# Windowed attention and SwiGLU on one core: blocks of tokens cut as 4 x 256 and 4 x 512 in place of 3 x 256, 4 x 512 and 256

## The chip, the cores and the metric

The kernel runs on one core of a Trainium2 chip. The metric is the device time of one execution in microseconds (us), lower is better. Before the change it is 239.15 us, the median of 5 runs (238.95 to 239.62). The engines are named as the profile names them: PE (TensorE matmul, with its weight loads PEld), DVE (VectorE), ACT (ScalarE), POOL (GpSimd) and SP (SyncE). POOL and SP issue the DMAs here.

## What is computed

Sliding-window attention with four sink tokens, and then a SwiGLU block over all tokens. Batch 4, 8 heads, 768 tokens, head size 64; model width 512, inner width 1536.

```python
scores = scale * np.matmul(q, k.transpose(0, 1, 3, 2))
is_sink = pos[None, :] < int(n_sink)                 # n_sink = 4
in_window = (rel >= 0) & (rel < int(window))         # window = 128
scores = np.where(is_sink | in_window, scores, -1e9)
a = softmax(scores)                                  # over the keys
x = (a @ v).transpose(0, 2, 1, 3).reshape(B * S, H * D)   # 3072 x 512
g = x @ w_gate
out = (g * sigmoid(g) * (x @ w_val)) @ w_out         # 3072 x 512, float32
```

## The kernel before

**Groups and blocks.** The attention works on groups of 256 tokens, three to a batch, so g = 0 to 11; `c = g % 3` is the place in the batch, and a group with c = 0 has no earlier window and no sink part. The SwiGLU block works on blocks of tokens, `SIZES`, with `OFF` their first tokens. Before, block 0 is group 0, block 1 group 1, block 2 group 2, blocks 3 to 6 are pairs of groups from (3, 4) to (9, 10), and block 7 is group 11.

**Units.** The program is a list of units that `weave` runs in order. A `gate` unit makes a `pg` (gate) and a `pv` (value) projection of 512 columns into PSUM, `project` at L417. ACT takes the tanh (`th`, L432), DVE makes `u` (L438) and `ht` (L440, L444). For a block of 512 tokens a unit is one of 12 chunks of the inner width, and `pg` is 4 matmuls of 512 columns. For a block of 256 tokens it is two chunks side by side, and `pg` is 8 matmuls of 256 columns. Blocks 0 and 1 share one `xT` and one `ht` tile, so that from chunk 6 on they run as one block "01" of 512 tokens. The weights arrive chunk by chunk, which is why the first block begins narrow. A `down` unit makes 128 output tokens in 12 matmuls (`pd`, L475); ACT copies them out of PSUM (`ot`, L480), and SP issues the store (L483).

**Attention steps** are hung into units by `slots`: a pair ((units), [steps]) says in which unit a step stands. In a gate unit the steps stand between `pg` and `pv`, in a down unit they are spread between its matmuls. What they leave for DVE or SP to do (`later`) is issued after the step or at the unit's end.

- `load_nat(g)`, `load_v(g)`: POOL loads q, k and v of a group with four and two DMAs of 128 KB. `NV` is both. From group 4 on `nat` has a single buffer, so the next group's loads wait until the crossbar has read the last.
- `xbar(g)`: four transposes of q and k by DMA, issued on SP (L259), for groups 4 to 11. `step_TN(g, i, j)` does the same on PE for groups 2 and 3 (`pn`, L245), and ACT or DVE copies the result out of PSUM.
- `step_S(g, p2)`: half of a group's scores, 12 matmuls (8 where c = 0) into four PSUM banks; four exponentials on ACT (L299), two masks on DVE. `step_K(g)`: scores of the sink tokens (`pk`), with one exponential `es`.
- `step_PV(g, j, hh)`: a quarter of a group's attention output (`o`, L355); the first quarter carries the sinks' four matmuls (L335) where c > 0. DVE normalizes to `xn` (L363, L369).
- `step_X(g, j)`: the transpose of 128 tokens of `xn` into the block's `xT`. Groups in `PEX` do it on PE (`px`, L396) with a copy by ACT or DVE (L399, L403). The others do it by DMA on SP (L391), "the crossbar".
- `step_ks(b)`, `step_vsb(b)`: the sink tokens' keys and values of a batch.

**Order.** Each engine runs its instructions in the order in which the program lists them, and SP's queue too: crossbar transposes of q and k, of `xn`, and the stores of the outputs stand in one line there. PSUM has eight banks for everything, `xT` three buffers, `ht` two.

**The first weave** has 24 units: group 0's and 1's narrow gates (units 0 to 5), six wide gates "01" (6 to 11), six narrow gates of block 2 (12 to 17), two down units each of blocks 0, 1 and 2 (18 to 23). Within it stand the attention of groups 2, 3 and 4, the transposes `xbar` 4 to 6 and the loads up to group 7. Then each of blocks 3, 4 and 5 is a weave of 12 gate and 4 down units in which `pair` hangs two groups of attention: (5, 6), (7, 8), (9, 10). The last weave holds blocks 6 and 7, with group 11's attention in block 6.

Of the kernel before, what the change touches and what calls it, by code (L numbers as in the profile page):

```python
# [8 lines left out]
BF16 = mybir.dt.bfloat16  # L9
# [5 lines left out]
def kernel(  # L15
# [12 lines left out]
    nc = tc.nc  # L28
    P = 128
# [7 lines left out]
    DMC = DM // P  # L37
    DFC = DF // P
    NP2 = H // 2
    GC = S // 256  # L40
    NG = B * GC
    SIZES = [256, 256, 256, 512, 512, 512, 512, 256]
    assert sum(SIZES) == NTOK and NG == 12
    OFF = [sum(SIZES[:i]) for i in range(len(SIZES))]
    PEX = (0, 1, 2, 4)

    VS = 72
    FCH = [2] * 6
# [4 lines left out]
    def pool(name, bufs, psum=False):  # L53
        if psum:
            return ctx.enter_context(
                tc.tile_pool(name=name, bufs=bufs, space=bass.MemoryType.PSUM))
        return ctx.enter_context(tc.tile_pool(name=name, bufs=bufs))
# [11 lines left out]
    xtp = pool("xtp", 3)  # L69
# [8 lines left out]
    def bank(shape, dtype, name):  # L78
        return psum.tile(shape, dtype, tag="b", name=name)
# [24 lines left out]
    def load_nat(g):  # L104
        b, c = divmod(g, GC)
        x = (natp if g > 3 else rowp).tile(
            [P, 2, 2, DM], BF16, tag="nat" if g > 3 else "rows", name="nat")
        for i, src in ((0, k), (1, q)):
            for j in range(2):
                t0 = c * 256 + j * P  # L110
                nc.gpsimd.dma_start(  # L111
                    x[:, i, j].rearrange("p (h d) -> p h d", d=D),
                    src[b, :, t0:t0 + P].rearrange("h p d -> p h d"))
        nats[g] = x
# [22 lines left out]
    def load_out(i):  # L137
        n = DFC // 4
        t = wpool.tile([P, n, DM], BF16, tag=f"wo{i}", name="wo")
        nc.gpsimd.dma_start(  # L140
            t, moe_w_out[i * n * P:(i + 1) * n * P].rearrange("(c p) f -> p c f", p=P))
        wos.append(t)
# [6 lines left out]
    vcl = const.tile([P, B - 1, D + 1], FP32)  # L149
# [57 lines left out]
    kTs, qTs, es_t, e_t, xns, xTs = {}, {}, {}, {}, {}, {}  # L207
    later = []

    def flush():  # L210
        for f in later:
            f()
        later.clear()
# [159 lines left out]
        else:  # L373
            later.append(dve)

    def dense(t, c, n):
        return t[:, 0:c * n].rearrange("p (c n) -> p c n", c=c)

    def step_X(g, j, evict="v"):
        t0 = g * 256 + j * P  # L380
        tb = max(i for i in range(len(SIZES)) if OFF[i] <= t0)
        off = t0 - OFF[tb]
        if tb == 0 and off == 0:
            xTs["01"] = xtp.tile([P, DMC, 512], BF16, tag="xT", name="xT")
            xTs[0], xTs[1] = (xTs["01"][:, :, 256 * i:256 * (i + 1)] for i in range(2))
        elif tb > 1 and off == 0:
            xTs[tb] = dense(xtp.tile([P, DMC * 512], BF16, tag="xT", name="xT"),
                            DMC, SIZES[tb])
        if g not in PEX:
            def sp():  # L390
                nc.sync.dma_start_transpose(xTs[tb][:, :, off:off + P], xns[g, j])  # L391
            later.append(sp)
            return
        pt = bank([P, DMC, P], BF16, "px")
        for i in range(DMC):
            nc.tensor.transpose(pt[:, i], xns[g, j][:, i * P:(i + 1) * P], ident)  # L396

        if evict == "a":
            nc.scalar.copy(out=xTs[tb][:, :, off:off + P], in_=pt)  # L399
            return  # L400

        def dve():
            nc.vector.tensor_copy(out=xTs[tb][:, :, off:off + P], in_=pt)  # L403
        if evict == "now":
            dve()
        else:
            later.append(dve)

    hts = {}
# [11 lines left out]

    def gate_a(tb, f):
        if tb not in hts:
            n = SIZES[tb]
            t = hpool.tile([P, DFC * 512], BF16, tag="ht", name="ht")
            hts[tb] = dense(t, DFC, n)
            if tb == 0:
                hts["01"] = t.rearrange("p (b c n) -> p b c n", b=2, c=DFC)
                hts[1] = t[:, DFC * n:2 * DFC * n].rearrange("p (c n) -> p c n", c=DFC)
        pg = project(wgs, tb, f, "pg")  # L430
        th = tpool.tile([P, 512], FP32, tag="th", name="th")
        nc.scalar.activation(th, pg, AF.Tanh, scale=0.5)  # L432
        return pg, th

    def gate_b(tb, f, pg, th):
        pv = project(wvs, tb, f, "pv")
        u = upool.tile([P, 512], BF16, tag="u", name="u")
        nc.vector.scalar_tensor_tensor(u, th, 1.0, pg, op0=ALU.add, op1=ALU.mult)  # L438
        if tb == "01":
            nc.vector.tensor_tensor(  # L440
                hts[tb][:, :, f], *(x.rearrange("p (b n) -> p b n", b=2) for x in (u, pv)),
                op=ALU.mult)
            return
        nc.vector.tensor_tensor(  # L444
            hts[tb][:, f:f + 512 // SIZES[tb]].rearrange("p a n -> p (a n)"), u, pv,
            op=ALU.mult)
# [42 lines left out]
    def gates(tb):  # L489
        return [(gate, tb, f) for f in range(0, DFC, 512 // SIZES[tb])]  # L490

    def downs(tb):
        return [(down, tb, t) for t in range(SIZES[tb] // P)]

    def A(fn, *a):
        return lambda: fn(*a)

    def TN(g, evict="av"):
        return [A(step_TN, g, i, j, evict) for j in range(2) for i in range(2)]

    def Ss(g):
        return [A(step_S, g, p2) for p2 in range(2)]

    def PVs(g):
        return [A(step_PV, g, j, hh) for hh in range(2) for j in range(2)]

    def Xs(g):
        return [A(step_X, g, j) for j in range(2)]

    def K(g):  # L510
        return A(step_K, g)

    def weave(us, slots):
        assert all(i < len(us) for i in slots)
        for i, (fn, tb, x) in enumerate(us):
            fn(tb, x, slots.get(i, []))
# [7 lines left out]
    def slots(*pairs):  # L524
        sl = {}
        for at, steps in pairs:
            for i, step in zip(at if isinstance(at, tuple) else (at,) * len(steps),
                               steps):
                sl.setdefault(i, []).append(step)
        return sl  # L530
# [79 lines left out]
    load_gate(4)  # L610
    load_gate(5)
    for i in range(4):
        load_out(i)
    step_T(1, 0, 0, "a")
    step_T(1, 0, 1, "a")
# [15 lines left out]
    step_S(1, 1)  # L631
    later[:0] = masks1
    flush()
    load_nat(3)
    load_v(3)
    nc.gpsimd.memset(vcl, 0.0)
    nc.gpsimd.memset(vcl[:, :, D:D + 1], 1.0)
    load_sinks(vcl, 1, B)

    g0, g1, g2 = gates(0), gates(1), gates(2)  # L640
    us = [g0[0], g0[1], (alone, 0, 0), (both, g0[2][1:], g1[0][1:]), g1[1],
          g1[2], *((gate, "01", f) for f in range(6, DFC)),
          *g2, *downs(0), *downs(1), *downs(2)]

    def L(*fs):
        def f():
            for x in fs:
                x()
        return f

    def NV(g):
        return L(A(load_nat, g), A(load_v, g))
# [5 lines left out]
        ((4, 4, 5, 5), TN(2)), ((6, 7), Ss(2)), (6, [K(2)]),  # L658
        ((8, 8), PVs(2)[:2]), (9, [A(step_PV, 2, 0, 1, "a"), A(step_PV, 2, 1, 1, "a")]),
        ((10, 11), [A(step_X, 2, 0, "a"), A(step_X, 2, 1, "a")]),  # L660
        (11, [NV(4), lambda: nc.gpsimd.tensor_copy(out=vcl[64:128], in_=vcl[0:64])]), ((14, 14, 15, 15), TN(3, "aa")),
        (15, [A(xbar, 4)]), (15, [NV(5)]), (19, [A(xbar, 5)]), (19, [NV(6)]),
        (23, [A(xbar, 6)]), (23, [NV(7)]),
        ((17, 18), Ss(3)), (18, [A(step_ks, 1)]), (18, [A(step_vsb, 1)]),
        ((19, 19, 19, 20), PVs(3)), (20, Xs(3)),
        ((19, 20), Ss(4)), (19, [K(4)]),
        ((21, 21, 22, 22), PVs(4)), (22, Xs(4))))

    def pair(ga, gb, sh=0):
        s = sh  # L670
        return [((s, s + 2), Ss(ga)), (s, [K(ga)]),
                ((s + 4, s + 5, s + 6, s + 7), PVs(ga)),
                ((s + 6, s + 8), Ss(gb)), ((s + 8, s + 9), Xs(ga)), (s + 6, [K(gb)]),
                ((12, 12, 13, 13) if s else (10, 10, 11, 12), PVs(gb)),
                ((14, 14) if s else (12, 13), Xs(gb))]

    weave(gates(3) + downs(3), slots(
        (2, [A(xbar, 7)]), (2, [NV(8)]),
        (15, [A(step_ks, 2), A(step_vsb, 2)]), *pair(5, 6),
        (15, [A(xbar, 8)]), (15, [NV(9)])))  # L680
    weave(gates(4) + downs(4), slots(
        *pair(7, 8), (3, [A(xbar, 9)]), (15, [A(step_ks, 3), A(step_vsb, 3)]),
        (3, [NV(10)]), (15, [A(xbar, 10)]), (15, [NV(11)])))
    weave(gates(5) + downs(5), slots(*pair(9, 10), (6, [A(xbar, 11)])))
    us = gates(6) + gates(7) + downs(6) + downs(7)
    us[-1] = (lambda tb, t, a: down(tb, t, a, True), *us[-1][1:])
    weave(us, slots(
        ((0, 2), Ss(11)), (0, [K(11)]), ((4, 5, 6, 7), PVs(11)), ((8, 9), Xs(11))))


# [33 lines left out]
```

## Time and profile before

The profile is of one execution. Its time was 239.15 us, its span from the first to the last instruction 237.3 us.

| what | busy, us | instructions |
|---|---|---|
| PE | 229.5 | 1874 |
| DVE | 158.5 | 335 |
| ACT | 114.5 | 237 |
| POOL | 74.5 | 98 |
| `pg` and `pv`, L417 | 73.1 and 73.0 | 351 and 351 |
| `pd`, L475 | 64.8 | 291 |
| `u` and `ht` on DVE | 49.2 and 49.5 | 72 and 72 |

Busy time is the union of an engine's instructions. A page divides the span into 40 slices and gives each engine's share in a slice as a digit from 0 to 9. A group's line has the source line, engine and operation, then output<-inputs with shapes and a count, then the busy time in us, the mean of one in ns, and the idle time just before them with what ended it. Matmuls overlap, so that the mean of one is longer than the distance between two. Some matmul records are missing. Software DMAs (POOL's) took 74.7% of the DMA engines' time, SP's 25.4%.

Places in the span that the text comes back to: group 2's gates begin at 43.40 us, the first output tile at 55.31, block 3 at 75.74, block 4 at 111.64, block 5 at 148.69, block 6 at 184.47, block 7's gates at 208.03, the last six output tiles at 218.51.

### The profile page before, as it was taken

How to read it: one execution, taken by the hardware profiler on the slowest of the kernel's cores; microseconds unless marked ns; L12 is line 12 of the kernel's file. 1: busy time of each engine (PE TensorE's matmuls, PEld its weight loads, DVE VectorE, ACT ScalarE, POOL GpSimd, SP SyncE). 2: the span in 40 equal slices, each digit the busy share in tenths (PEclk: the TensorE clock that was granted, in tenths of full speed). 3: DMA queues.
4: the chain of work that ended last, by engine and by line, in shares of the span. 5: the costliest groups of instructions: out<-in, count | busy, mean ns of one | idle time of the engine just before them, and what ended most of it. 6: DMA issues, size and time to landing. Idle time of an engine off the chain costs nothing.

```text
span 237.3 us, 4886 instructions
## 1 busy us (share of the span) xinstructions
PE 229.5 (97%) x1874; PEld 127.1 (54%) x1901; DVE 158.5 (67%) x335; ACT 114.5 (48%) x237; POOL 74.5 (31%) x98
## 2 busy tenths in 40 slices
PE   8899999999999999999999999999999999999994
PEld 4577845795554444444444444444444445488443
DVE  5888778768652888970798980688970598877000
ACT  4896485467452835512845622655622663333221
POOL 8995864720708026260261700080000000000000
DMA  7999999993999959999499994599204100200132
GB/s 137 159 179 177 180 201 204 158 147 72 133 140 177 195 112 125 142 131 204 111 129 108 121 68 145 137 98 133 44 20 139 64 3 0 44 3 1 51 128 88
DMA packets 107655, 27.36 MB, mean 115 GB/s; under 512 B 94704, under 2 KB 104688, under 8 KB 107632
## 3 DMA queue, kind: packets, MB, share of 16 engines
q0 software_dynamic: 76640, 13.90, 74.7%
q1 hardware_dynamic: 30448, 12.89, 25.4%
q8 instruction: 15, 0.25, 0.4%
q10 hardware_dynamic: 544, 0.26, 0.4%
q14 instruction: 8, 0.07, 0.1%
HBM read 28.34 MB, written 6.29 MB: 146 GB/s over the span
## 4 chain that ended last, share of the span: by engine, by line
PE 88%; ACT 4%; DMA 2%; POOL 2%; issue 2%; DVE 2%; POOLq 0%; DVEq 0%; ACTq 0%
PE pd L475 26%; PE pv L417 26%; PE pg L417 25%; PE o L355 4%; PE s L292 4%; DMA va<-in_v_dram 2%; ACT e L299 2%; POOL rows L100 1%; PE pn L245 1%; ACT xn L366 1%; POOL x L188 1%; PE o L335 1%; PE pk L320 1%; ACT th L432 1%; DVE u L438 1%
## 5 line engine op out<-in xcount | busy, mean ns | idle before, releaser
L438 DVE SCALAR_TENSOR_TENSOR u<-th,pg 128x512 bf16<-128x512 f32 x72 | 49.2, 683 | 38.8 <-ACT th L432 38.8
L417 PE MATMUL pg<-xT,wg 128*128 128x512 bf16 (+1 forms) x351 | 73.1, 335 | 0.8
L417 PE MATMUL pv<-xT,wv 128*128 128x512 bf16 (+1 forms) x351 | 73.0, 336 | 0.8 <-DMA wv<-in_moe_w_val_dram 0.2
L432 ACT ACTIVATE th<-pg 128x512 f32<-128x512 f32 x72 | 43.5, 604 | 62.6 <-PE pg L417 58.8
L475 PE MATMUL pd<-wo,ht 128*128 128x512 bf16 (+2 forms) x291 | 64.8, 370 | 0.4
L444 DVE TENSOR_TENSOR ht<-u,pv 128x512 bf16<-128x512 bf16 x66 | 45.4, 688 | 10.4 <-PE pv L417 3.5
L417 PEld LDWEIGHTS <-wg 128*128 128x128 bf16 x360 | 34.9, 98 | 28.4 <-issue 1.2
L299 ACT ACTIVATE e<-s 128x512 bf16<-128x512 f32 (+1 forms) x88 | 42.7, 583 | 3.5 <-PE s L292 3.5
L475 PEld LDWEIGHTS <-ht 128*128 128x128 bf16 x300 | 27.9, 98 | 30.0 <-issue 0.5
L417 PEld LDWEIGHTS <-wv 128*128 128x128 bf16 x360 | 32.0, 98 | 21.0 <-issue 1.7
L111 POOL DMA_DIRECT2D nat<-in_k_dram x20 | 17.6, 887 | 76.3 <-DMA qT<-nat 73.4
L480 ACT ACTIVATE ot<-pd 128x512 f32<-128x512 f32 (+1 forms) x24 | 14.3, 596 | 47.4 <-PE pd L475 43.4
L304 DVE TENSOR_TENSOR e<-e,mask 128x1024 bf16<-128x1024 bf16 (+1 forms) x44 | 27.3, 655 | 4.0 <-ACT e L299 4.0
L122 POOL DMA_DIRECT2D va<-in_v_dram x24 | 21.5, 917 | 4.5 <-DMA wo<-in_moe_w_out_dram 2.5
L369 DVE TENSOR_TENSOR xn<-o,rcp 128x256 bf16<-128x256 f32 x44 | 18.7, 425 | 1.5
L355 PEld LDWEIGHTS <-e 128*128 128x128 bf16 x352 | 15.0, 98 | 7.9 <-DVE lt L603 0.4
L111 POOL DMA_DIRECT2D nat<-in_q_dram x20 | 17.6, 893 | 0.9 <-DMA wv<-in_moe_w_val_dram 0.4
L355 PE MATMUL o<-va,e 128*128 128x65 bf16 x352 | 17.0, 193 | 0.3 <-DMA va<-in_v_dram 0.2
L292 PE MATMUL s<-qT,kT 64*128 64x128 bf16 (+1 forms) x240 | 12.9, 237 | 0.0
L292 PEld LDWEIGHTS <-kT 64*128 64x128 bf16 x240 | 7.7, 94 | 7.6 <-issue 6.6
L482 DVE TENSOR_SCALAR ot<-pd 128x128 f32<-128x128 f32 x1 | 0.3, 292 | 14.3 <-PE pd L475 14.3
L363 DVE RECIPROCAL rcp<-o 128x4 f32<-128x4 f32 x48 | 8.1, 175 | 1.5 <-PE o L355 1.5
(73 smaller groups left out, 92.6 us busy)
## 6 DMA issues: line engine op xcount, KB each, us to landing
out_dram<-ot SPq DMA_DIRECT2D x23, 256.0 KB
va<-in_v_dram POOLq DMA_DIRECT2D x24, 128.0 KB, 6.2
nat<-in_k_dram POOLq DMA_DIRECT2D x20, 128.0 KB, 4.7
nat<-in_q_dram POOLq DMA_DIRECT2D x20, 128.0 KB, 5.4
wg<-in_moe_w_gate_dram POOLq DMA_DIRECT2D x6, 256.0 KB, 7.9
wv<-in_moe_w_val_dram POOLq DMA_DIRECT2D x6, 256.0 KB, 8.4
wo<-in_moe_w_out_dram POOLq DMA_DIRECT2D x4, 384.0 KB, 11.6
st<-in_k_dram SPq DMA_DIRECT2D x2, 128.0 KB
```

The costliest lines, as they stand in the source:

```text
L111: nc.gpsimd.dma_start(x[:, i, j].rearrange("p (h d) -> p h d", d=D), src[b, :, t0:t0 + P].rearrange("h p d -> p h d"))
L122: nc.gpsimd.dma_start(va[:, j, :, 0:D], v[b, :, t0:t0 + P].rearrange("h p d -> p h d"))
L292: nc.tensor.matmul(pss[2 * pp + h][:, col:col + n], kTs[b][r, p, kk:kk + P], qTs[b][r, p, qq:qq + n], start=True, stop=True)
L299: nc.scalar.activation(e_t[g][:, h0 + h, lo:512], pss[2 * pp + h][:, lo:512], AF.Exp, scale=scale)
L304: nc.vector.tensor_tensor(e, e, m[:, :, lo:512].broadcast_to([P, 2, 512 - lo]), op=ALU.mult)
L355: nc.tensor.matmul(o, l, r, start=(c == 0 and i == 0), stop=(i == len(mms) - 1), skip_group_check=True)
L369: nc.vector.tensor_tensor(xn, po[:, :, 0:D], rcp.broadcast_to([P, 4, D]), op=ALU.mult)
L417: nc.tensor.matmul(ps[:, i * n:(i + 1) * n], ws[fi][:, c, fo * P:(fo + 1) * P], xTs[tb][:, c], start=(c == 0), stop=(c == DMC - 1))
L432: nc.scalar.activation(th, pg, AF.Tanh, scale=0.5)
L438: nc.vector.scalar_tensor_tensor(u, th, 1.0, pg, op0=ALU.add, op1=ALU.mult)
L444: nc.vector.tensor_tensor(hts[tb][:, f:f + 512 // SIZES[tb]].rearrange("p a n -> p (a n)"), u, pv, op=ALU.mult)
L475: nc.tensor.matmul(po, hts[tb][:, f, ts * P:(ts + 1) * P], wos[f // n][:, f % n, lo:hi], start=(f == 0), stop=(f == DFC - 1))
```

## The change

Block 7's 256 tokens and block 2's are put together in a different way: there are four blocks of 256 (groups 0 to 3) and four of 512 (pairs from (4, 5) to (10, 11)). Groups 2 and 3 now run as 0 and 1 do: narrow for chunks 0 to 5, as one wide block from chunk 6 on. The first weave has 32 units: 0 to 11 as before, two narrow gates of group 2, then four down units of blocks 0 and 1, then the third narrow gate of group 2 and three of group 3, six wide gates, four down units of blocks 2 and 3. The attention of groups 3, 4 and 5 stands in it, and `pair` hangs (6, 7), (8, 9) and (10, 11) into the next three blocks. The last block has no attention. The transposes of group 3's q and k stand in one unit where they stood in two. Group 3's attention output is transposed on PE, group 4's by the crossbar. The loads of group 3's q and k go ahead of the last two loads of `w_out`, and several `xbar` and load steps stand in other units.

```diff
-    SIZES = [256, 256, 256, 512, 512, 512, 512, 256]
+    SIZES = [256] * 4 + [512] * 4
-    PEX = (0, 1, 2, 4)
+    PEX = (0, 1, 2, 3)
...
-        if tb == 0 and off == 0:
-            xTs["01"] = xtp.tile([P, DMC, 512], BF16, tag="xT", name="xT")
-            xTs[0], xTs[1] = (xTs["01"][:, :, 256 * i:256 * (i + 1)] for i in range(2))
-        elif tb > 1 and off == 0:
-            xTs[tb] = dense(xtp.tile([P, DMC * 512], BF16, tag="xT", name="xT"),
-                            DMC, SIZES[tb])
+        if tb not in xTs:
+            x = xtp.tile([P, DMC, 512], BF16, tag="xT", name="xT")
+            if tb < 4:
+                xTs[tb, tb + 1] = x
+                xTs[tb], xTs[tb + 1] = x[:, :, 0:256], x[:, :, 256:512]
+            else:
+                xTs[tb] = x
...
     for i in range(4):
+        if i == 2:
+            load_nat(3)
         load_out(i)
...
-    load_nat(3)
     load_v(3)
...
-    us = [g0[0], g0[1], (alone, 0, 0), (both, g0[2][1:], g1[0][1:]), g1[1],
-          g1[2], *((gate, "01", f) for f in range(6, DFC)),
-          *g2, *downs(0), *downs(1), *downs(2)]
+    us = [g0[0], g0[1], (alone, 0, 0), (both, g0[2][1:], g1[0][1:]), g1[1], g1[2],
+          *wide(0, 6), *g2[:2], *downs(0), *downs(1), g2[2], *g3[:3], *wide(2, 6),
+          *downs(2), *downs(3)]
...
-        (11, [NV(4), lambda: nc.gpsimd.tensor_copy(out=vcl[64:128], in_=vcl[0:64])]), ((14, 14, 15, 15), TN(3, "aa")),
-        (15, [A(xbar, 4)]), (15, [NV(5)]), (19, [A(xbar, 5)]), (19, [NV(6)]),
-        (23, [A(xbar, 6)]), (23, [NV(7)]),
-        ((17, 18), Ss(3)), (18, [A(step_ks, 1)]), (18, [A(step_vsb, 1)]),
-        ((19, 19, 19, 20), PVs(3)), (20, Xs(3)),
-        ((19, 20), Ss(4)), (19, [K(4)]),
-        ((21, 21, 22, 22), PVs(4)), (22, Xs(4))))
+        (11, [NV(4), lambda: nc.gpsimd.tensor_copy(out=vcl[64:128], in_=vcl[0:64])]),
+        ((13, 13, 13, 13), TN(3, "aa")), ((14, 15), Ss(3)), (14, [A(xbar, 4), NV(5)]),
+        (16, [A(step_ks, 1), A(step_vsb, 1)]),
+        ((16, 16), PVs(3)[:2]), ((17, 17), PVs(3)[2:]), (17, [A(step_X, 3, 0)]),
+        (18, [A(step_X, 3, 1, "a")]),
+        ((17, 19), Ss(4)), (17, [K(4)]), (18, [A(xbar, 5), NV(6)]),
+        ((20, 21, 22, 23), PVs(4)), ((23, 25), Ss(5)), (23, [K(5)]),
+        ((24, 25), Xs(4)), (25, [A(xbar, 6), NV(7)]),
+        ((27, 27, 28, 28), PVs(5)), ((29, 30), Xs(5)), (31, [A(xbar, 7), NV(8)])))
...
-    weave(gates(3) + downs(3), slots(
-        (2, [A(xbar, 7)]), (2, [NV(8)]),
-        (15, [A(step_ks, 2), A(step_vsb, 2)]), *pair(5, 6),
-        (15, [A(xbar, 8)]), (15, [NV(9)])))
     weave(gates(4) + downs(4), slots(
-        *pair(7, 8), (3, [A(xbar, 9)]), (15, [A(step_ks, 3), A(step_vsb, 3)]),
-        (3, [NV(10)]), (15, [A(xbar, 10)]), (15, [NV(11)])))
-    weave(gates(5) + downs(5), slots(*pair(9, 10), (6, [A(xbar, 11)])))
-    us = gates(6) + gates(7) + downs(6) + downs(7)
+        (2, [A(step_ks, 2), A(step_vsb, 2)]), *pair(6, 7), (3, [A(xbar, 8), NV(9)]),
+        (15, [A(xbar, 9), NV(10)])))
+    weave(gates(5) + downs(5), slots(
+        *pair(8, 9), (3, [A(xbar, 10), NV(11)]), (15, [A(xbar, 11)]),
+        (15, [A(step_ks, 3), A(step_vsb, 3)])))
+    weave(gates(6) + downs(6), slots(*pair(10, 11)))
+    us = gates(7) + downs(7)
     us[-1] = (lambda tb, t, a: down(tb, t, a, True), *us[-1][1:])
-    weave(us, slots(
-        ((0, 2), Ss(11)), (0, [K(11)]), ((4, 5, 6, 7), PVs(11)), ((8, 9), Xs(11))))
+    weave(us, {})
```

`gate_a` makes `ht` in the same way as `step_X` makes `xT`: one tile for two blocks below 4. `gate_b` takes its branch for a wide block of two where `tb` is a tuple. `pair` loses its argument `sh`, which was 0 in every call.

## Prediction

> **What bounds the kernel.** I read the page's busy shares first, then its groups kept apart by shape, the busy time by stage, the timeline of PE, ACT and DVE around the first outputs, and last the landings of SP's transfers. From the page:
>
> ```profile
> PE 229.5 (97%) x1874; PEld 127.1 (54%) x1901; DVE 158.5 (67%) x335; ACT 114.5 (48%) x237; POOL 74.5 (31%) x98
> PE   8899999999999999999999999999999999999994
> DMA  7999999993999959999499994599204100200132
> PE 88%; ACT 4%; DMA 2%; POOL 2%; issue 2%; DVE 2%; POOLq 0%; DVEq 0%; ACTq 0%
> ```
>
> PE is full from the second slice to the last; the chain of waits is PE for 88%, its rest almost all before 22 us. DMA is full for half the span. A busy PE is not yet proof, as ends of matmuls are modelled, so I also took distances between starts: four 512-wide matmuls of `pg` start 0.86 us before the next group, four times 0.216. That is a packed stream. So time can come from PE's work, or from holes in it. The groups by shape give the widths that the change exchanges:
>
> ```profile
> L417 PE MATMUL pg<-xT,wg 128*128 128x512 bf16 x207 | 54.5, 379 | 0.6
> L417 PE MATMUL pg<-xT,wg 128*128 128x256 bf16 x144 | 18.7, 273 | 0.2
> L417 PE MATMUL pv<-xT,wv 128*128 128x256 bf16 x144 | 18.5, 273 | 0.2 <-DMA wv<-in_moe_w_val_dram 0.2
> ```
>
> A mean of 273 against 379 ns looks as if two narrow ones cost 44% more than a wide one. They overlap: in the timeline eight narrow ones last 0.873 us from group to group, four wide ones 0.8635. This is the price, 0.01 us in 0.87.
>
> The busy time by stage, cut at 43.40 (group 2's projections begin), 75.74, 111.64, 148.69 (the three blocks with two groups of attention), 184.47 and 218.51 (the last outputs):
>
> ```profile
> 43.40:75.74 32.34, 31.87 (x297) 20.49 (x300) 20.28 (x46) 15.76 (x32) 13.48 (x17) 1.00 1.50 132
> 75.74:111.64 35.90, 35.53 (x247) 17.02 (x253) 25.35 (x53) 16.51 (x33) 12.27 (x15) 1.00 1.45 156
> 111.64:148.69 37.05, 36.61 (x276) 17.72 (x280) 25.37 (x53) 17.48 (x34) 10.51 (x12) 1.00 1.11 114
> 148.69:184.47 35.78, 35.52 (x248) 17.02 (x252) 24.08 (x48) 16.59 (x33) 5.25 (x6) 1.00 0.71 96
> 218.51:237.30 18.79, 15.62 (x84) 7.71 (x83) 1.62 (x3) 3.48 (x6) 0.00 (x0) 1.00 0.24 85
> ```
>
> Columns: stretch, its length, busy PE, PEld, DVE, ACT, POOL, clock, DMA. PE has 0.2 to 0.5 us free in each. The clock is 1.00 throughout. So little is to be won, and the change must be judged by holes it makes.
>
> **PE's work, step by step.** Up to 43.40 PE's order is the same. From there until the first block without 256-wide halves, in starts: TN 8 transposes 0.45; S of a batch's first group 0.44 a half, of others 0.55; K 0.23; sinks 0.22; a PV quarter 0.25 (0.12 for a batch's first 128 tokens); px 0.22; a down tile 12 x 0.2157 = 2.59; and about 0.10 at each change from a full-height matmul to S, K or sinks (a `pg` group before S lasts 0.96).
>
> Before: 12 x 0.873 + 6 x 2.59 + TN 0.90 + S 0.88 + 1.10 + K 0.23 + sinks 0.22 + PV 1.74 + px 0.44 + 6 x 0.10 = 32.1, of 32.34 measured: holes of 0.2 only.
> After: 12 x 0.873 + 12 x 0.8635 + 8 x 2.59 + TN 0.90 + S 0.88 + 2.20 + K 0.46 + sinks 0.44 + PV 2.74 + px 0.44 + 9 x 0.10 = 50.5, so without holes this part ends at 93.9.
> Then the blocks with groups (6,7), (8,9), (10,11), at the same slots as before's pairs. (6,7) is like (9,10), a batch's first group and a second one: 35.78. (8,9) is like (5,6): 35.90. (10,11) is like (7,8): 37.05. The last block has no attention: 24 x 0.8635 = 20.72. Its outputs and the end: 18.79 less two tiles, 13.61.
> Sum 43.40 + 50.51 + 143.06 = 236.97 us, against 237.30: 0.33 less (0.11 from the widths, 0.22 from holes that went). That is all the change can bring by this reckoning.
>
> **The holes it makes**, each at a place where PE, in order, meets something late.
>
> 1. All four TN of group 3 stand in one 256-wide unit (from 45.14), evicted by ACT. ACT's tanh starts at 46.22; the timeline shows eviction starts 0.49 after a tanh and 0.46 after each other, so the fourth ends about 48.70. S(3,0) is now three `pd` into the next tile, due at 48.54. Cost 0.2. Before, two units lay between.
> 2. Group 3's second px is in unit g2[2], its ACT copy ahead of g3[0], the next unit, which reads it. ACT's queue: S(4,0) due at 59.65, its exps from 60.07, 0.48 apart, es 61.99, output copy 62.15, tanh 62.63, xT copy 63.12 to 63.77. PE is ready for g3[0] at about 63.36. Cost 0.45. The same sequence stands in the trace: group 2's second copy ended 43.35, `pg` began 43.40, a hole of 0.3 in a `pv` group of 1.16 for 0.86.
> 3. `wo` is due 8 us earlier (47.8 for 55.3). Landings before: `wo` 37.7, 39.6, 41.6, 43.5, then nat(3) until 47.1. With nat(3) ahead of the last two, nat(3) lands by 43.3 (due 46.0), the last `wo` by 47.1 (due 50). Cost 0; POOL has the same bytes up to there.
> 4. Crossbar of group 4: last piece landed 58.20, S(4,0) due 59.65, with no store ahead on SP. Cost 0.
> 5. Crossbar of group 5: it stands on SP behind four stores (one before); the fourth waits for the output copy that ends at 62.8, while nat(5) landed from 62.7. So SP loses 0.5. Nat(5) to last piece took 58.76 to 71.69; S(5,0) is due at 73.8. Cost 0, cover 2 us.
> 6. PSUM around that S: in block (5,6) a PV and an S waited about 0.17 for DVE's xn. Units 19 to 27 are a bit denser (three S halves and six PV in nine units). Between 0 and 0.3; I take 0.1.
> 7. X of group 5 by the crossbar, due at the block's start, 94.65. Its second half stands on SP behind the store of the tile before. Output copy ends 90.2, store 0.4, transpose until 91.9, then the landing. Rows of before: 1.2 after the issue's end where DMA is quiet, 3.67 and 4.00 where nat(8) was loading. At 91.9 nat(7) and va(7) are loading to about 93.5 to 94.7. Between 0 and 1.2; I take 0.1, since landings in such stretches followed the loads' end by 0.3.
>
> ```profile
> 103.62 1.19 SPq L391 DMA_TRANSPOSE xT<-xn  x1
> 104.94 0.49 SPq L483 DMA_DIRECT2D out_dram<-ot  x1
> 105.54 1.26 SPq L391 DMA_TRANSPOSE xT<-xn  x1
> ```
>
> Here a rule speaks otherwise. The Trainium skill, "Advanced Engine Details and Errata", section "X-Bar Transpose (TRN2)", says "TRN2 transpose DMAs are as fast as regular DMAs". By it the transpose would hold SP 0.4 us as the store, and the data be in place by 92.7 in a quiet stretch: no hole. The row says 1.2 us on SP for half of the store's bytes. By the row an exchange of PE transposes for the crossbar costs SP three times a store, and step 7 stays open. I use the row.
>
> The other exchange (X of group 4 by crossbar, of group 3 on PE) is 8 transposes for 8 and nothing on PE. Group 4's second transpose now stands behind group 6's crossbar on SP, lands about 85, due 94.65: hidden by 9 us. The later crossbars are earlier than before by their blocks' reckoning: group 7's is issued at the block's start, 94, due 107.
>
> Holes 0.2 + 0.45 + 0.1 + 0.1 = 0.85. Span 237.82. The profiled execution took 239.15, 1.85 more than its span, and is itself the median of the runs. **Forecast 239.7 us**, 0.2% slower, at the edge of what a measurement tells from no change (0.2%, 0.48 us).
>
> **Rivals.**
> - *The small waits hide* (chance 0.25): ACT is ahead. It is busy 15.76 of 32.34 us there, which speaks for it; its order, four exps and three more ahead of the xT copy, against. It decides whether that copy ends before PE is through g2[2] (63.36). Then 236.97 + 1.85 = 238.8, up to 239.1 with one of them left: not slower.
> - *The crossbar is late* (0.27): more stores beside nat(5), and step 7's landing. Nat(6), with three stores beside it, took 14.9 us from its issue to the last piece (nat(5) 12.9), nat(4) 16.3 under the weights' backlog. 58.76 + 14.9 = 73.7 is just in time, 58.76 + 16.3 = 75.1 is 1.3 late. Step 7 at worst 1.2. Half of both: 241.0; all of it: 242.1.
> - *The forecast's own case* (0.48) spans 239.2 to 240.3 by the bounds of steps 1, 2, 6, 7; most of it lies above 239.63.
>
> Slower by over 0.2%: 0.27 and 0.25 of the 0.48, 0.52. Within 0.2%: the rest of it and most of the first rival, 0.35. Faster: what the sum doesn't know, 0.13. Range 238.6 to 241.5.
>
> **What would show it.** Eight-matmul groups at 0.873, four-matmul ones at 0.86, and 96 matmuls fewer of width 256 for 48 of 512. A `pg` of g3[0] that starts just after an ACT xT copy. The first S of group 3 released by ACT's kT or qT copy. S(5,0) without a DMA ahead of it, and the first `pg` of the block of groups 4 and 5 within 0.5 us of the last `pd`. It would be wrong if that block began later than 95.5 in the span, or if a pair block lasted 0.5 us longer or shorter than its like.

## The result, and the profile after

The changed kernel took 239.72 us (median of 29 runs, 239.19 to 245.73), the kernel before 239.15 us (median of 50). The ratio is 1.0024, with a 95% interval from 1.0014 to 1.0034: slower by a quarter of a per cent. Runs over 1.5% above the fastest of the same kernel are left out of every ratio; here that is the one of 245.73, at a mean granted clock of 0.992, and the next slowest took 240.89. The profiled run took 239.64 us with a span of 237.9, at a clock of 1.00.

The page of the changed kernel, in the same four lines as before (busy shares, PE and DMA by slices, the chain of waits by engine):

```profile
PE 229.5 (97%) x1826; PEld 123.5 (52%) x1853; DVE 156.8 (66%) x334; ACT 115.2 (48%) x238; POOL 74.5 (31%) x98
PE   8998999999999999999999999999999999999994
DMA  8999999997979999599995499995500204200022
PE 80%; DVE 5%; POOL 4%; DMA 3%; ACT 3%; issue 2%; DVEq 0%; POOLq 0%; ACTq 0%
```

PE has 48 matmuls fewer and is as full as before. Its share of the chain fell from 88 to 80%, which looks like 19 us of new waits. It is not: the chain now starts with another load at the front (8.2 us of `wv` instead of 5.4 of `va`), and it steps aside onto other engines, as onto mask multiplications by DVE at 97.8 and 102.2, while PE works on. Where the share went can't be read as a loss; distances between starts on PE tell it. The groups kept apart by shape (count, then busy time and mean of one, then idle time before them):

```profile
L415 PE MATMUL pg<-xT,wg 128*128 128x512 bf16 x231 | 60.5, 379 | 0.4
L415 PE MATMUL pg<-xT,wg 128*128 128x256 bf16 x96 | 12.5, 273 | 0.5 <-ACT xT L397 0.3
L292 PE MATMUL s<-qT,kT 64*128 64x256 bf16 x88 | 10.6, 270 | 0.2 <-ACT qT L249 0.2
```

48 narrow matmuls went and 24 wide ones came for `pg`, and the two idle entries name two ACT copies that PE now waits for. The busy time by stage, cut 0.3 to 0.45 us after the starts of the blocks (stretch, length, PE, PEld, DVE, ACT, POOL, clock, DMA, GB/s):

```profile
43.40:94.90 51.50, 50.53 (x435) 29.61 (x442) 31.91 (x70) 24.99 (x51) 19.59 (x23) 1.00 1.52 154
94.90:131.00 36.10, 35.66 (x251) 17.09 (x254) 24.68 (x53) 16.76 (x34) 10.50 (x12) 1.00 1.25 119
131.00:166.90 35.90, 35.53 (x249) 17.02 (x253) 24.76 (x52) 16.51 (x34) 10.51 (x12) 1.00 1.14 118
166.90:203.90 37.00, 36.56 (x276) 17.69 (x280) 24.63 (x48) 17.44 (x35) 0.00 (x0) 1.00 0.21 54
```

The first stretch has 0.97 us without PE work, the three others 0.37 to 0.44 each, near what their likes had before (0.26 to 0.44). So the loss is in the first. In starts of PE's groups: 43.38, 94.61, 130.55, 166.46 and 203.50, then 34.4 us to the end.

The two places, first ACT's timeline of the changed kernel (start, length), then PE's:

```profile
46.70 0.58 ACT L249 COPY kT<-pn 128x512 bf16<-128x512 bf16 x1
...
48.11 0.63 ACT L249 COPY qT<-pn 128x512 bf16<-128x512 bf16 x1
...
60.12 2.06 ACT L299 ACTIVATE e<-s 128x512 bf16<-128x512 f32 x4 [2.04 <-PE s L292]
62.04 0.31 ACT L324 ACTIVATE es<-pk 128x128 bf16<-128x128 f32 x1
62.20 0.65 ACT L478 ACTIVATE ot<-pd 128x512 f32<-128x512 f32 x1
62.67 0.66 ACT L430 ACTIVATE th<-pg 128x512 f32<-128x512 f32 x1
63.15 0.66 ACT L397 COPY xT<-px 128x512 bf16<-128x512 bf16 x1
```

```profile
43.38 1.03 PE L415 MATMUL pg<-xT,wg 128*128 128x256 bf16 x8
...
48.80 0.51 PE L292 MATMUL s<-qT,kT 64*128 64x256 bf16 x8 [0.22 <-ACT qT L249]
...
63.86 1.03 PE L415 MATMUL pg<-xT,wg 128*128 128x256 bf16 x8 [0.29 <-ACT xT L397]
...
94.61 1.03 PE L415 MATMUL pg<-xT,wg 128*128 128x512 bf16 x4
```

The fourth q,k copy ends at 48.74 and S(3,0) starts 0.06 later; the xT copy ends at 63.81 and g3[0] starts 0.05 later. The brackets show only part of each hole, because the end of the group ahead is modelled late (a `pv` group lasted 1.32 for 0.87). Measured against runs in which they are gone (below), from start to start, the holes are 0.29 and 0.45 us.

### The profile page after: what moved, and what is told of

The parts are those of the page before. It is cut to its first block, busy times and chain, and to the rows that moved or that the text cites. A ratio compares the mean times of both kernels' runs of the same rounds, so it can differ in the third digit from the quotient of the medians.

```text
span 237.9 us, 4793 instructions
## 1 busy us (share of the span) xinstructions
PE 229.5 (97%) x1826; PEld 123.5 (52%) x1853; DVE 156.8 (66%) x334; ACT 115.2 (48%) x238; POOL 74.5 (31%) x98
## 4 chain that ended last, share of the span: by engine, by line
PE 80%; DVE 5%; POOL 4%; DMA 3%; ACT 3%; issue 2%; DVEq 0%; POOLq 0%; ACTq 0%
PE pd L473 25%; PE pv L415 23%; PE pg L415 23%; PE o L355 4%; DMA wv<-in_moe_w_val_dram 3%; PE s L292 3%; DVE u L436 2%; POOL va L122 1%; DVE ht L442 1%; POOL rows L100 1%; ACT e L299 1%; ACT th L430 1%; DVE e L304 1%; PE o L335 1%; POOL x L188 1%
## 5 line engine op out<-in xcount | busy, mean ns | idle before, releaser
L415 PEld LDWEIGHTS <-wg 128*128 128x128 bf16 x336 | 32.6, 98 | 30.7 <-issue 1.3
L442 DVE TENSOR_TENSOR ht<-u,pv 128x512 bf16<-128x512 bf16 x60 | 41.3, 688 | 9.8 <-PE pv L415 3.6
L415 PEld LDWEIGHTS <-wv 128*128 128x128 bf16 x336 | 29.7, 97 | 24.3 <-issue 1.7
L478 ACT ACTIVATE ot<-pd 128x512 f32<-128x512 f32 (+1 forms) x24 | 14.3, 595 | 49.1 <-PE pd L473 47.1
L355 PEld LDWEIGHTS <-e 128*128 128x128 bf16 x352 | 14.9, 98 | 7.5 <-DVE lt L601 0.3
L438 DVE TENSOR_TENSOR ht<-u,pv 128x512 bf16<-128x512 bf16 x12 | 8.3, 688 | 2.1 <-PE pk L320 0.7
```

Of the source, the lines that this page charges most:

```text
L355: nc.tensor.matmul(o, l, r, start=(c == 0 and i == 0), stop=(i == len(mms) - 1), skip_group_check=True)
L415: nc.tensor.matmul(ps[:, i * n:(i + 1) * n], ws[fi][:, c, fo * P:(fo + 1) * P], xTs[tb][:, c], start=(c == 0), stop=(c == DMC - 1))
L442: nc.vector.tensor_tensor(hts[tb][:, f:f + 512 // SIZES[tb]].rearrange("p a n -> p (a n)"), u, pv, op=ALU.mult)
```

## The experiments

All but one are edits of the changed kernel. PE's starts are compared from the start of group 2's projections (43.38 in the changed kernel's profile), since that start itself lies anywhere from 43.1 to 44.2 in the profiles; differences are of unrounded times. Ratios are against the kernel before, measured alongside (its medians lay between 239.09 and 239.56).

| run | edit | median us (runs) | ratio, 95% interval | span, clock |
|---|---|---|---|---|
| e2_tn_av | copies of hole 1 on two engines | 239.98 (14) | 1.0031, 1.0007 to 1.0055 | 238.1, 0.999 |
| e1_x31_dve | copy of hole 2 on DVE | 244.19 (6) | 1.0195, 1.0159 to 1.023 | 243.9, 0.985 |
| e3_both | both | 243.61 (6) | 1.0127, 1.0081 to 1.0173 | 242.1, 0.993 |
| e4_three | both, and group 2's copy on DVE | 243.95 (6) | 1.0145, 1.0105 to 1.0185 | 243.3, 0.986 |
| e5_x5_later | group 5's xT one unit later | 240.88 (6) | 1.0071, 1.0046 to 1.0096 | 238.7, 1.00 |
| e6_x5_pe | group 5's xT by PE | 240.61 (9) | 1.0053, 1.0035 to 1.0072 | 239.2, 1.00 |
| e7_nat3_late | nat(3) behind all of `wo` | 240.20 (11) | 1.0043, 1.0026 to 1.0059 | 238.6, 1.00 |
| e8_before_x21 | kernel before, group 2's copy on DVE | 239.02 (22) | 0.9995, 0.9984 to 1.0006 | 237.3, 1.00 |
| e9_both_early | both, group 5's xT one unit earlier | 239.28 (14) | 0.9995, 0.9977 to 1.0013 | 237.1, 1.00 |
| e10_both_nat2 | both, two buffers for nat | 248.02 (6) | 1.031, 1.0261 to 1.0359 | 243.2, 0.984 |
| e11_both_early_nat2 | all of these | 243.82 (6) | 1.015, 1.0118 to 1.0182 | 242.1, 0.993 |
| e12_both_xb5 | both, group 5's q,k transposes ahead of a store | 239.24 (16) | 1.0002, 0.9978 to 1.0025 | 243.2, 0.993 |

### The two holes, filled

Hole 1, the four q,k copies shared by ACT and DVE:

```diff
-        ((13, 13, 13, 13), TN(3, "aa")),
+        ((13, 13, 13, 13), TN(3)),
```

> Only the copies of group 3's k and q transposes are shared by ACT (k) and DVE (q), as group 2's are. Theory A: the hole of 0.26 us before the first S of group 3 goes and nothing else moves: span 237.6 to 237.7, ratio about 1.0015. Theory B: no change of the span beyond 0.1 us.

Hole 2, the second xT copy of group 3 on DVE:

```diff
-        (18, [A(step_X, 3, 1, "a")]),
+        (18, [A(step_X, 3, 1, "now")]),
```

> Only the copy of group 3's second px moves from ACT to DVE, ahead of u. Theory A (the change's loss is two holes of PE behind ACT's queue): the hole of 0.45 us before g3[0] goes, as DVE has a free 0.4 us there; the first projection of g3[0] begins 0.87 us after the px, and the span is 237.4 to 237.5, ratio to before about 1.0005. Theory B (the crossbar's lateness or the denser attention costs the time): the hole goes, but comes back at S of group 5 or at the block of groups 4 and 5, whose xT landed 0.2 us before its use: span above 237.7, ratio above 1.0015.

Both, and both with the same edit for group 2's second copy (unit 11, `"a"` to `"now"`):

> Both edits together. Theory A: span 237.1 to 237.2, just below before's 237.3; ratio 0.9985 to 1.0005. Step 7 of the prediction is then nearest to deciding: xT of group 5 is issued on SP after a store that moves earlier with PE by 0.7 us, so its landing should move too unless DMA's backlog sets it; if the backlog sets it, up to 0.4 us come back at the first projection of the block of groups 4 and 5. Theory B: ratio stays above 1.0015.

> Both edits, and group 2's second px copy on DVE too, where before and after alike have a hole of 0.31 us. Theory A: 0.3 us less than with both edits: span about 236.9, ratio about 0.9980, below before by 0.2%, if the crossbar of groups 3 to 5 still lands in time. Theory B: no gain over the two edits, since the crossbar's chain of loads and transposes does not start earlier.

Each hole goes when its copy is early. From group 2's start, S(3,0) comes at 5.13 instead of 5.41 us in e2_tn_av (0.29 earlier), and g3[0] at 20.03 instead of 20.48 in e1_x31_dve (0.45). S(3,0) of e2_tn_av, whose group 2 starts at 43.35, and g3[0] of e1_x31_dve, whose group 2 starts at 43.29:

```profile
48.47 0.50 PE L292 MATMUL s<-qT,kT 64*128 64x256 bf16 x8
```

```profile
63.32 1.04 PE L415 MATMUL pg<-xT,wg 128*128 128x256 bf16 x8
```

But no time was won. In e2_tn_av, block 4 starts at 51.17 after group 2 instead of 51.23: group 5's xT lands at 94.43 and its first `pg` starts at 94.52, so 0.23 of the 0.29 was given back at the next transfer. In e1_x31_dve much more than the gain was lost. Its PE at the start of block 4, SP's issue of the second half of group 5's xT, then its busy time by stage:

```profile
91.70 2.54 PE L473 MATMUL pd<-wo,ht 128*128 128x512 bf16 x11
97.40 1.86 PE L415 MATMUL pg<-xT,wg 128*128 128x512 bf16 x4 [3.16 <-issue]
```

```profile
90.14 1.34 SPq L389 DMA_TRANSPOSE xT<-xn  x1
```

```profile
70.00:96.50 26.50, 24.02 (x178) 11.64 (x180) 14.99 (x34) 10.03 (x19) 10.51 (x12) 1.00 1.27 114
96.60:103.40 6.80, 6.00 (x21) 2.05 (x22) 2.21 (x4) 2.13 (x5) 1.38 (x2) 0.50 0.97 173
```

"Issue" says that the profile shows no releaser. The landings do: that second half was complete at 97.31, 5.83 us after its issue (2.49 in the changed kernel), and PE started 0.09 later. From 96.62, within that standstill, the granted clock is 0.5 for 6.83 us. The account closes: 3.16 us of waiting and 3.4 of half clock, less 0.45, is 6.1; the span grew by 6.0. e3_both waits 2.97 us at the same place and has 3.41 us at 0.5, and e4_three has 6.83 us at 0.5; the third copy does not help.

### How much room the transfer had

Group 5's xT one unit later (its first half then goes where the second was), and on PE instead of the crossbar:

```diff
-        ((27, 27, 28, 28), PVs(5)), ((29, 30), Xs(5)),
+        ((27, 27, 28, 28), PVs(5)), ((30, 31), Xs(5)),
```

> Group 5's two crossbar transposes of its output stand one down unit later. Step 7's theory: the second waits on SP for the store of the next tile, is issued at about 93.3 and done issuing at 94.5, lands 1.2 to 2.5 us later; the first projection of the block begins at 95.7 to 97.0 for 94.61: 1.1 to 2.4 us slower than the change. If the landing were hidden by several us (rival: it has slack), no change.

```diff
-    PEX = (0, 1, 2, 3)
+    PEX = (0, 1, 2, 3, 5)
```

> Group 5's output is transposed on PE. If the crossbar's landing held up the block (rival: the crossbar is late), this is no slower than the change. If it was in time by 0.2 us, it costs PE eight transposes, 0.44 us, and no more: span about 238.3.

PE of e5_x5_later at the start of block 4:

```profile
95.50 1.02 PE L415 MATMUL pg<-xT,wg 128*128 128x512 bf16 x4 [1.02 <-issue]
```

One unit later costs 1.2 us in starts (52.41 against 51.23 after group 2), the low end of what was expected, since the landing was quiet by then: 1.21 us after the issue's end. With the transposes on PE, block 4 starts 51.67 after group 2, 0.44 later: the price of two px and nothing else. So in the changed kernel the crossbar was in time and cost PE nothing. Its cover was just 0.2 us: landed 94.40, needed 94.61, and PE started 0.09 us after the landing in the runs where it waited for it (e1_x31_dve, e2_tn_av, e5_x5_later). That cover is what the two filled holes eat.

### Two smaller questions

nat(3) put back behind all four `wo`, where it had stood:

> Group 3's q and k are loaded after all four w_out loads, as before the change. Their landings were 44.4 to 47.1 us then; the transposes of group 3 are due at 46.0, the last needs the last load. Theory: PE waits about 0.5 to 1 us at the transposes, and about 0.3 more at the first S as ACT's copies follow later: 0.5 to 1.3 us slower than the change. If the move of the loads were idle: no change.

The `pn` group lasts 1.17 instead of 0.89, a hole of 0.28, below what was expected; and S(3,0) comes 5.41 after group 2 as before, since it waits for ACT's copies anyway. Block 4 stands at 51.23, the same. So with hole 1 there, moving nat(3) won nothing in this profile. Its span is 0.7 longer because its group 2 starts at 44.18; whether the edit does that isn't settled, and the ratios' intervals overlap.

The kernel before has a hole of the second kind too (group 2's second copy, 0.3 us). The same edit there:

```diff
-        ((10, 11), [A(step_X, 2, 0, "a"), A(step_X, 2, 1, "a")]),
+        ((10, 11), [A(step_X, 2, 0, "a"), A(step_X, 2, 1, "now")]),
```

> The kernel before, with group 2's second px copy on DVE in place of ACT. The hole of 0.31 us before group 2's first narrow projection goes: span about 237.0, ratio 0.9987, if nothing behind it takes the time back. This tells whether the third edit is worth the same without the change.

A miss: no gain. DVE's timeline of that run shows why:

```profile
42.24 0.69 DVE L440 TENSOR_TENSOR ht<-u,pv 128x512 bf16<-128x512 bf16 x1
42.84 0.42 DVE L403 COPY xT<-px 128x512 bf16<-128x512 bf16 x1
43.20 0.67 DVE L438 SCALAR_TENSOR_TENSOR u<-th,pg 128x512 bf16<-128x512 f32 x1
```

The transposes are done by about 42.2, but DVE is busy with `ht` until 42.9, so its copy ends at 43.26 and `pg` starts at 43.31, where ACT's copy had ended at 43.35. A copy moved to the other engine waits in that engine's queue.

### Where the late transfer comes from

The delay can be followed back. POOL's loads of nat(6) and nat(7), of the changed kernel and then of e1_x31_dve:

```profile
70.29 1.75 POOL L111 DMA_DIRECT2D nat<-in_k_dram  x2 [7.66 <-DMA qT<-nat]
...
82.61 1.75 POOL L111 DMA_DIRECT2D nat<-in_k_dram  x2 [7.06 <-DMA qT<-nat]
```

```profile
71.85 1.76 POOL L111 DMA_DIRECT2D nat<-in_k_dram  x2 [9.80 <-DMA qT<-nat]
...
86.90 1.75 POOL L111 DMA_DIRECT2D nat<-in_k_dram  x2 [9.79 <-DMA qT<-nat]
```

Nat has one buffer, so nat(6) may be loaded only when the last of group 5's four q,k transposes is down. In e1_x31_dve that transpose leaves SP at 68.37, 0.16 earlier than in the changed kernel; 15 of its 16 pieces are there 1.22 us later, but the last takes 2.93 (1.21 in the changed kernel). So nat(6) starts 1.6 us later. Group 6's transposes then wait for these loads, the last of them is down at 86.34 instead of 82.06, and nat(7) starts 4.3 later. Its loads are then in flight when group 5's xT needs the DMA engines.

What delays the one piece? Each profile has a 16 KB instruction fetch nearby (the DMA queue that the page calls `instruction`). The table gives by how much it starts ahead of the 15th piece's landing:

| profile | fetch starts | 15th piece lands | ahead by | last piece after the issue's end | nat(6) |
|---|---|---|---|---|---|
| changed kernel | 69.62 | 69.73 | 0.11 | 1.21 | 70.29 |
| e2_tn_av | 69.82 | 69.43 | not ahead | 1.27 | 69.99 |
| e5_x5_later | 69.26 | 69.39 | 0.13 | 1.26 | 69.99 |
| e6_x5_pe | 70.31 | 70.07 | not ahead | 1.20 | 70.63 |
| e7_nat3_late | 70.38 | 70.52 | 0.14 | 1.22 | 71.08 |
| e1_x31_dve | 69.12 | 69.58 | 0.46 | 2.93 | 71.85 |
| e3_both | 69.41 | 69.84 | 0.43 | 3.00 | 72.19 |
| e4_three | 69.52 | 69.97 | 0.45 | 2.86 | 72.09 |
| e9_both_early | 69.00 | 69.46 | 0.46 | 2.98 | 71.78 |
| e12_both_xb5 | 68.89 | 69.40 | 0.50 | 2.72 | 71.49 |

The other transposes say the same. In all 14 profiles, 345 crossbar transposes had 15 pieces down within 1.45 us of the issue's end. In the 330 of them that met no such fetch, the last piece was never more than 0.08 us behind. Fifteen met one. In all nine where it started 0.43 to 0.63 us ahead, the last piece came 1.53 to 1.78 us behind; of the six where it started 0.10 to 0.14 ahead, one did (e12_both_xb5, group 6). Two of the nine are in the kernel before, and one of these is the last q,k transpose of group 4.

Counted from group 2's start, the fetch comes 0.38 to 0.71 us earlier than in the changed kernel in the five profiles with a late piece, where PE is 0.45 to 0.74 ahead; in e2_tn_av it comes 0.23 later though PE is 0.29 ahead. That PE running ahead brings the fetch into the transpose fits all rows with a late piece. It is not shown by itself, as no run moved the fetch alone.

The next runs ask whether the late xT is what costs, whatever made it late:

```diff
-        ((27, 27, 28, 28), PVs(5)), ((29, 30), Xs(5)),
+        ((27, 27, 28, 28), PVs(5)), ((28, 29), Xs(5)),
```

> The two copies to DVE, and group 5's crossbar transposes of its output one down unit earlier, so that the second stands on SP ahead of the store that it waited for. Theory C (new: with the holes filled PE runs 0.5 us ahead, its 16 KB instruction fetch at 69.1 us meets the last crossbar piece of group 5 on one DMA engine, 2.93 us to land for 1.22; the next group's loads start 1.6 us later, group 7's 4.3 us, and these are in flight when xT of group 5 is transposed, which lands 3.2 us late; PE stands still that long and its clock is then halved for 6.8 us): the transpose leaves 2.5 us earlier, lands about 95.0 to 94.0, PE waits under 1 us and the clock stays at 1.0: span 237.2 to 238.0, ratio 1.000 to 1.003. Theory D (a fuller PE is throttled by itself): the clock falls below 1.0 and the span stays above 241.

PE's timeline of e9_both_early, SP's issue of the second half of xT, and the stage:

```profile
91.77 2.32 PE L473 MATMUL pd<-wo,ht 128*128 128x512 bf16 x10
93.93 1.03 PE L415 MATMUL pg<-xT,wg 128*128 128x512 bf16 x4
```

```profile
87.84 1.23 SPq L389 DMA_TRANSPOSE xT<-xn  x1
```

```profile
43.40:93.90 50.50, 50.00 (x433) 29.39 (x440) 33.02 (x73) 23.45 (x47) 19.67 (x24) 1.00 1.41 141
```

The wait is gone although the last transpose piece is as late as in e3_both (2.98 us) and nat(6) as late (71.78): xT is issued 2.5 us earlier (until 89.07 instead of 91.60 in e3_both) and lands at 92.96, 1.0 ahead of its use. Block 4 starts 50.49 us after group 2, 0.74 less than in the changed kernel, which is both holes. The clock stays at 1.00, against theory D. This version undoes the change's loss: its ratio to the kernel before is 0.9995, 0.9977 to 1.0013. It is the best form of the change found here, and it does not beat the kernel before. The earlier xT was not run without the two copies.

Two buffers for nat, so that no load waits for a transpose, in two versions:

```diff
-    natp = pool("natp", 1)
+    natp = pool("natp", 2)
```

> The two copies to DVE, and two buffers for q and k as loaded (natp), so that a group's loads no longer wait for the crossbar of the group before. Theory C: loads of group 7 end before 80 us, the transposes of group 5's output run in a quiet stretch, 1.2 us to land, no wait at the block: clock 1.0, span 237.1 to 237.3, ratio 0.999 to 1.0005. A remainder of theory C: loads of group 8 take the place of group 7's beside these transposes; then up to 1 us. Theory D: clock below 1.0, span above 241.

> All four edits. Theory C: clock 1.0, no wait at the block, span 237.0 to 237.2: ratio 0.998 to 1.000, the level that the prediction's sum without holes gives (236.97). Theory D: clock below 1.0, span above 241.

Both missed. PE of e10_both_nat2:

```profile
59.01 0.23 PE L292 MATMUL s<-qT,kT 64*128 64x128 bf16 x2
61.88 0.93 PE L292 MATMUL s<-qT,kT 64*128 64x256 bf16 x10 [2.64 <-DMA qT<-nat]
```

The loads no longer wait, so nat(5) is in flight from 48.9 to 60, beside group 4's transposes, and S(4,0), which waits for its transposes in none of the runs with one buffer, stands 2.64 us; the clock is 0.5 for 6.83 us from 61.24. In e11_both_early_nat2 it stands 1.64 us, and the clock is 0.5 for 3.41 us from 62.98. The one buffer was a brake that kept loads off the crossbar.

Last, group 5's four q,k transposes ahead of the store they stood behind:

```diff
-        ((17, 19), Ss(4)), (17, [K(4)]), (18, [A(xbar, 5), NV(6)]),
+        ((17, 19), Ss(4)), (17, [K(4)]), (17, [A(xbar, 5), NV(6)]),
```

> Edit: the two earlier copies (the first k,q transposes of the prologue on both copy engines, X(3,1)'s copy on VectorE) as in the run with both, and on SyncE the four q,k transposes of block 5 one unit earlier, so that they stand ahead of the store they stood behind. Theory F (with the two earlier copies TensorE runs half a microsecond ahead, so a 16 KB instruction fetch at about 69.1 to 69.4 falls on the last of these four transposes; one DMA engine finishes it 1.7 us late, the next group's q,k load starts 1.5 us late, and that delay grows until block 4 stands still for 3 us and the clock drops): now the last transpose is down by about 69.0 to 69.3, before or just at the fetch; its last piece lags by 1.3 us at most, the load of group 6 is issued by 70.2, block 4 waits less than 0.5 us, granted clock 1.0, span 237.1 to 237.6, ratio 0.998 to 1.002. Rival G (the delay comes from the earlier copies in another way, by the engines' order or the store): the load of group 6 still starts near 72, block 4 waits about 3 us, clock below 1, ratio above 1.010.

SP's timeline of that run, and PE's:

```profile
61.56 1.19 SPq L259 DMA_TRANSPOSE kT<-nat  x1
64.40 1.19 SPq L259 DMA_TRANSPOSE qT<-nat  x1
...
66.99 1.22 SPq L259 DMA_TRANSPOSE qT<-nat  x1
68.30 0.53 SPq L481 DMA_DIRECT2D out_dram<-ot  x1
```

```profile
98.03 1.61 PE L415 MATMUL pg<-xT,wg 128*128 128x512 bf16 x4 [4.00 <-issue]
```

The edit did less than meant: only the first transpose left earlier (61.56 instead of 63.43 in e3_both), the second then stood until 64.40, and the last left at 66.99 as in e9_both_early (67.03). The profiled run took 245.02 us, with the late piece, a wait of 4.00 us and a clock of 0.993. That is what G expected of nat(6) and of the wait, but the run does not decide against F: the fetch still started 0.50 us ahead of the piece. Nor does the ratio look like G's: 9 of the 16 runs took 238.49 to 239.25, the other seven 240.05 to 245.02, and the mean of all 16 is 1.0044 times that of the kernel before. The same kernel goes either way from run to run, as it would with a transfer that has almost no cover; that the good runs lack the late piece could not be seen, as they have no trace. The fetch is the likely cause by the count above; shown it is not.

## Why the prediction was right

The forecast was 239.7 us by its own case; 239.72 was measured. The loss is where it was put, at two ACT copies in the first weave. That the two numbers agree to 0.02 us is luck, as errors of up to 0.2 us in single terms cancelled. The terms, each against the trace:

- **PE's work.** Without holes the stretch from group 2 to block 4 was reckoned at 50.51. The changed kernel took 51.23 with 0.74 of holes, which leaves 50.49; e9_both_early, without the holes, took 50.49. Eight narrow matmuls take 0.873 and four wide ones 0.8635 in the new order too. The blocks lasted 35.94, 35.91 and 37.04 for 35.78, 35.90 and 37.05; the last and the end 34.36 for 34.33. The 0.16 of the first block is one wait: a `pv` at 108.48 stands for DVE's `xn`, the kind of wait that step 6 looked for at S(5,0).
- **Steps 1 and 2**, the two holes: the fourth copy ended at 48.74 (forecast about 48.70) and the xT copy at 63.81 (63.77). The holes measured 0.29 (0.2) and 0.45 (0.45). That the copy's place in ACT's queue makes them is shown by e2_tn_av and e1_x31_dve, where each goes.
- **Step 3.** nat(3) landed at 42.86 (forecast by 43.3) and the last `wo` at 46.77 (47.1): no hole. e7_nat3_late shows that the old order costs 0.28 at the transposes, which hole 1 swallows.
- **Step 4.** Group 4's q,k was down at 56.82, better than 58.20: no wait.
- **Step 5** had the right sign and too small a cover. The last piece landed at 69.74, not at 71.7, mostly since nat(5) started 1.4 us earlier (57.38 for 58.76): 4 us of cover instead of 2. Those 1.4 us were luck: in the kernel before, the last piece of group 4's transposes was a late one, 1.53 us behind the others, and in the changed kernel it was not. The error hid, as the cover did not decide.
- **Step 6**, PSUM at S(5,0): forecast 0.1, measured none.
- **Step 7**, group 5's xT: forecast 0.1 within 0 to 1.2; measured none, by 0.2 us. SP's lines of the changed kernel:

```profile
90.26 0.33 SPq L481 DMA_DIRECT2D out_dram<-ot  x1
90.68 1.23 SPq L389 DMA_TRANSPOSE xT<-xn  x1
```

  The store holds SP 0.33 us and the transpose 1.23 for half its bytes, the row that was set against the rule of equal speed (its words are of the DMA's speed; that it also sets how long SP is held was the prediction's reading). It landed 2.49 after its issue, between the 1.2 and the 3.67 of the rows. That this was the sore spot was right; that it could cost far more than 1.2 was not seen: 3.2 us of standstill, and as much again by the clock, once PE is half a microsecond earlier.

Steps 6 and 7 were 0.2 too high, the blocks and the end 0.18 too low, hole 1 0.09 too low and the rest 0.03 too high, so the sum came out at 237.82 for 237.85. The first rival, that the small waits hide, is refuted by the two brackets; the second, that the crossbar is late, did not happen in the profiled run, and happened in e1_x31_dve, e3_both, e4_three and e12_both_xb5. Whether it made the changed kernel's one run of 245.73 us can't be told, as that run has no trace. Of the rows that this rival was sized by, the two longest (16.3 and 14.9 us, of nat(4) and nat(6)) hold a last piece that came 1.53 and 1.66 us late.

## What to carry to other kernels

A hole can be read before it exists: write down what stands in the copying engine's queue ahead of the copy, and compare its end with when PE is ready. But before filling it, look at the cover of the next transfer behind it: a gain of 0.7 us ran into a transfer with 0.2 us to spare, and only moving that transfer one unit forward as well kept it. A single buffer that makes a load wait may be what keeps that load off a more urgent transfer; a second buffer here made two versions 1.5 and 1.8% slower.

## What the runs showed of the hardware that was not expected

- A standstill of PE costs more than itself. After standstills of 1.64 us (e11_both_early_nat2), 2.64 (e10_both_nat2), 2.97 (e3_both), 3.00 (e4_three), 3.16 (e1_x31_dve) and 4.00 (e12_both_xb5) the granted clock was 0.5 for 3.41, 6.83, 3.41, 6.83, 6.83 and 3.41 us, and a group of four wide matmuls took 1.7 us for 0.86; after 1.02 us (e5_x5_later) it stayed at 1.00. With half of each slow stretch counted as lost, they cost about 1.4 to 2.3 times their length. The stretches are one or two windows of 3.41 us, the length that the Trainium skill, "TensorE: Matmul & The Clock Gate", Part 1, gives; it names a whole idle window as the limit, and here less was enough: in the 3.41 us before the clock fell, PE had been busy for 0.29 (e12_both_xb5) to 1.63 us (e11_both_early_nat2).
- Beside the loads of q and k, the landing of one crossbar transpose of xT went from 1.2 us after its issue (e5_x5_later) to 2.49 (changed kernel), 5.83 (e1_x31_dve) and 6.74 (e12_both_xb5), where the stores beside it took up to 6.25.
- In ten of the 345 transposes whose other pieces landed within 1.45 us, one piece of sixteen came 1.5 to 2.0 us behind the others, each time with a 16 KB instruction fetch that had started 0.10 to 0.63 us before; the next load waited for that one piece.
